# Gradient of w_down by seven block products, T4 late, a fourth staging buffer in the last group, Y transposed in the dxn loop

## The chip, the cores and the metric

The kernel runs on one core of one Trainium2 chip. The time is device microseconds of one execution of the whole program; the number used for a kernel is the median of its runs. Before the change three runs gave 796.46, 795.10 and 795.39 us: median 795.39. One more execution was recorded by the profiler, and all views below are of that one.

## The reference

A layer of linear attention with 32 heads and a SwiGLU feed-forward, with residuals, and its gradient. S = 2048 tokens, D = 640, F = 1728, all inputs bf16:

```python
h  = x + A(layernorm(x), wqkv, wo)            # linear attention, phi(t) = t+1 or exp(t)
h2 = h + (silu(hn @ w_gate) * (hn @ w_up)) @ w_down     # hn = layernorm(h)
_out, _vjp = jax.vjp(f, x, wqkv, wo, w_gate, w_up, w_down)
return (_out, *_vjp(grad_out))                # out_0, then dx, dwqkv, dwo, dw_gate, dw_up, dw_down
```

In the feed-forward's backward part, with g = hn @ w_gate and u = hn @ w_up, the kernel needs m = silu(g) * u, the gradients dg and du, and from them dw_down = m^T @ dh2 (dh2 is grad_out), dw_gate = hn^T @ dg, dw_up = hn^T @ du and dhn = dg @ w_gate^T + du @ w_up^T.

## The kernel before

Tokens lie in 16 tiles of 128 rows; D is 5 blocks of 128. The program runs through stages: attention forward (ps_kvt, L534 among them), gradient through w_down (ps_dm, L417), then the **feed-forward backward stage**, then ps_dhn (L108, the gradient into hn), attention backward, the **dxn loop** (L1069) and the **tail** (out_0's product L1138, ps_dwv L127).

**The feed-forward backward stage** runs over four groups g = 0 to 3 of columns of F, of width w = 448, 448, 448 and 384. A group goes through eight pairs of token tiles, t = 0, 2, ... 14. Per pair PE makes pg (gate, L731) and pu (up, L736), 20 matmuls; ACT takes two sigmoids and two copies of them (L752 to L755); DVE's seven operations at L764 write m into m_s and [dg | du] into dd (dd[0] holds tiles 0 to 7, dd[1] tiles 8 to 15); for the last pair they stand in another order, with dg last. SP then transposes each token tile of dd into a staging buffer, stg (L767), and stores the buffer into scr_dT in DRAM (L720); a store is issued one tile behind its transpose. The staging buffers are three, in turn. SP also issues the loads of the next group's weights, wgu (L190); in group 0 that load is asked for at t = 2.

**dw_group** then makes the weight gradients of the group's w columns: dw_down (transposed, into scr_dwdT; the five row blocks of D against m_s), dw_gate and dw_up (the five row blocks of D against dd's two halves of columns). Before, all of dw_down and row block 4 of gate and up are plain products over 16 tiles, by dw() into PSUM tiles ps_dw (L806). Row blocks 0 to 3 of gate and up are one product of 2 x 2 blocks by the Strassen-Winograd scheme: seven block products (prod, L646) in place of eight. The blocks of hn are two row-block pairs by two token halves, hn_blk(m, k, u). The blocks of dd are B11 and B12 (gate and up columns of the first token half), B21 and B22 (second half). DVE makes the sums that it needs by tt (L642): S and S3 from hn (128 x 1024 elements each), and from dd the differences T1 = B12 - B11, T2 = B22 - T1, T3 = B22 - B12 and T4 = B21 - T2 (128 x 8w each). T1 and T2 overwrite B11, T3 overwrites B12; T4 is written into m_s, whose own products are done by then. Partial results go from PSUM to buffers by ACT (copy, L673) and DVE (tt), and from there to DRAM by POOL's queue.

Inside dw_group a manual schedule sets the order of PE, DVE and ACT as the code is written; SP's order is set by hand in the whole stage. An engine does its list in order. Outside, a scheduler interleaves: the first pg matmuls of the next group may stand ahead of the last product of dw_group.

After group 3, ps_dhn starts. It reads cols, four token tiles of scr_dT at a time, loaded by load_cols: before, load_cols(0) and load_cols(1) are both issued by ACT (L157), the first ahead of group 3's dw_group, the second behind it; the later ones are issued by POOL (L160).

**The dxn loop** runs over 16 token tiles. SP issues three transposes into a ring of tiles per iteration (L972, L973, L1044), read by PE's ps_dxn. At iterations 8 to 13 it issues one transpose more, of G from scr_GT (L938); at 14 that of KV (L1050), from 14 on the first ones of mT (L1028), which the tail reads. **In the tail** SP transposes the rest of mT and, two at a time between them, six pieces of Y from scr_Yt, which ps_dwv reads.

## Time and profile before

| | us |
|---|---|
| median of three runs | 795.39 |
| the profiled execution's own time | 795.63 |
| its span in the profile | 793.9 |
| group 0's weight gradients, first product to the next group's first pg | 172.25 to 214.62 |
| group 3's weight gradients, to the first ps_dhn | 401.03 to 437.43 |
| one iteration of the dxn loop | 5.43 |

What lies outside the span, 795.63 - 793.9 = 1.7 us, is start and end of the program. Every view is read in microseconds from the span's start. In the chain of work that ended last a row has its start, its length, the engine, the tile, the line and how many instructions it groups; in the groups of instructions, a row has the line, engine, operation, tiles with their shape, count, the busy time in all with the mean of one in ns, and the idle time before it. A matmul's row shows it from issue to its end, 346 ns at 448 columns; since they are pipelined, the pace in a stream is read from the length of a chain row over its count.

### The profile page before, as it was taken

The numbers are of one execution on the slowest core, as the hardware profiler recorded it, in microseconds if no ns is written. First come the engines' busy times: TensorE is split into PE (matmuls) and PEld (weight loads), VectorE is DVE, ScalarE is ACT, GpSimd is POOL, SyncE is SP. The second block draws the span as 40 slices with busy tenths as digits, with TensorE's granted clock in tenths as the row PEclk, the third lists the DMA queues.
The fourth block names the chain that finished last, engine by engine and source line by source line (L and its number), as shares of the span: only waits on it lengthen the run. The fifth ranks groups of instructions, "written<-read, shape, count | busy, mean of one in ns | idle before, by whom it ended". The sixth has DMA issues, their size and how long they took to land.

```text
span 793.9 us, 13612 instructions
## 1 busy us (share of the span) xinstructions
PE 788.4 (99%) x5308; PEld 509.0 (64%) x5308; DVE 568.2 (72%) x1014; ACT 288.0 (36%) x414; POOL 172.7 (22%) x306
## 2 busy tenths in 40 slices
PE   9999999999999999999999999999999999999998
PEld 7776566555555555555666777777777777777766
DVE  7989988894497548845875259999897366635873
ACT  6962532760284045501831123223313133324010
POOL 4610047411201110011042102111221121223230
PEclk9999999999999999999999999999999999999999
DMA  9799999999769977892797659876498869999995
GB/s 261 154 241 298 209 211 277 262 256 238 171 154 241 214 169 191 211 253 71 148 233 196 253 144 191 217 194 176 120 257 176 161 135 161 177 212 239 228 213 150
DMA packets 286625, 160.03 MB, mean 202 GB/s; under 512 B 241548, under 2 KB 275405, under 8 KB 286560
## 3 DMA queue, kind: packets, MB, share of 16 engines
q1 hardware_dynamic: 268832, 99.48, 61.7%
q0 software_dynamic: 14832, 54.36, 22.6%
q10 hardware_dynamic: 2896, 5.33, 2.0%
q8 instruction: 41, 0.67, 0.4%
q14 instruction: 24, 0.20, 0.1%
HBM read 47.60 MB, written 53.66 MB: 128 GB/s over the span
## 4 chain that ended last, share of the span: by engine, by line
PE 97%; SPq 1%; DMA 1%; DVE 0%; issue 0%
PE ps_dhn L108 15%; PE ps_dw L806 10%; PE ps_dxn L1069 8%; PE pg L731 7%; PE ps_wa L646 7%; PE pu L736 7%; PE ps_kq L305 6%; PE ps_dwqk L986 5%; PE ps_dm L417 5%; PE ps_oa L1138 3%; PE ps_wc L646 3%; PE ps_y L508 3%; PE ps_dk L108 3%; PE ps_gt L861 3%; PE ps_dp L108 3%; PE ps_a L571 3%
## 5 line engine op out<-in xcount | busy, mean ns | idle before, releaser
L108 PE MATMUL ps_dhn<-wgT,cols 128*128 128x320 bf16 x864 | 119.5, 299 | 0.0
L108 PEld LDWEIGHTS <-cols 128*128 128x128 bf16 x864 | 84.5, 98 | 32.9
L146 DVE CUSTOM_DVE_ANT_0 lb_a<-lb_dy,hn 128x640 bf16<-128x640 bf16 x32 | 26.4, 825 | 58.9 <-ACT lb_dy L144 58.9
L731 PE MATMUL pg<-wgu,hnT 128*128 128x448 bf16 (+1 forms) x320 | 63.6, 346 | 0.0
L736 PE MATMUL pu<-wgu,hnT 128*128 128x448 bf16 (+1 forms) x320 | 63.6, 346 | 0.0
L806 PE MATMUL ps_dw<-m_s,dh 128*128 128x448 bf16 (+1 forms) x320 | 60.4, 346 | 0.0
L1069 PEld LDWEIGHTS <-ring 128*128 128x128 bf16 x480 | 47.0, 98 | 18.2
L1069 PE MATMUL ps_dxn<-wqkvT,ring 128*128 128x320 bf16 x320 | 51.3, 299 | 0.0
L736 PEld LDWEIGHTS <-hnT 128*128 128x128 bf16 x320 | 31.3, 98 | 27.1
L806 PEld LDWEIGHTS <-dh 128*128 128x128 bf16 x320 | 31.3, 98 | 27.1
L731 PEld LDWEIGHTS <-hnT 128*128 128x128 bf16 x320 | 31.3, 98 | 27.0
L417 PEld LDWEIGHTS <-dh2T 128*128 128x128 bf16 x320 | 31.0, 98 | 25.1
L417 PE MATMUL ps_dm<-wdT,dh2T 128*128 128x448 bf16 (+1 forms) x240 | 46.5, 344 | 0.0
L144 ACT ACTIVATE lb_dy<-ps_dhn,rstd 128x640 bf16<-128x640 f32 x16 | 12.7, 794 | 91.7 <-PE ps_dhn L108 91.7
L305 PE MATMUL ps_kq<-wqk,xnT 128*128 128x320 bf16 x320 | 45.0, 300 | 0.0
L752 ACT ACTIVATE dd<-pg 128x896 bf16<-128x896 f32 (+1 forms) x32 | 28.5, 890 | 40.4 <-PE pg L731 38.0
L305 PEld LDWEIGHTS <-xnT 128*128 128x128 bf16 x320 | 31.2, 98 | 12.2 <-DVE xnT L352 0.2
L646 PEld LDWEIGHTS <-S 128*128 128x128 bf16 x256 | 25.0, 98 | 21.7
L772 POOL DMA_DIRECT2D scr_m<-m_s x16 | 12.1, 756 | 122.6 <-DVE m_s L764 122.6
L986 PEld LDWEIGHTS <-hn 128*128 128x128 bf16 x320 | 31.1, 98 | 11.9
L642 DVE TENSOR_TENSOR dd<-dd 128x3584 bf16<-128x3584 bf16 (+1 forms) x12 | 23.1, 1953 | 21.4 <-PE ps_wa L646 15.6
L150 ACT ACTIVATE lb_a<-hn,lb_k 128x640 bf16<-128x640 bf16 x32 | 29.5, 920 | 21.7 <-DVE lb_k L149 18.9
(205 smaller groups left out, 1524.7 us busy)
## 6 DMA issues: line engine op xcount, KB each, us to landing
scr_dT<-stg SPq DMA_DIRECT2D x48, 224.0 KB, 2.8
cols<-scr_dT POOLq DMA_DIRECT2D x6, 1728.0 KB, 8.6
scr_m<-m_s POOLq DMA_DIRECT2D x12, 448.0 KB, 4.7
cols<-scr_dT ACTq DMA_DIRECT2D x2, 1728.0 KB, 10.6
scr_dT<-stg SPq DMA_DIRECT2D x16, 192.0 KB, 2.2
scr_pq<-pqa SPq DMA_DIRECT2D x4, 640.0 KB, 4.4
scr_xnT<-xnT SPq DMA_DIRECT2D x4, 640.0 KB, 5.3
scr_pk<-pk SPq DMA_DIRECT2D x4, 640.0 KB, 4.5
```

The lines of the kernel that those rows point to most:

```text
L108: nc.tensor.matmul(ps[:, ci, :320], lhsT=lhs(k), rhs=rhs(k, *NCH[ci]), start=(start and k == 0), stop=(stop and k == n - 1))
L146: nc.vector.tensor_tensor_reduce(out=a[:], in0=dy[:], in1=xhat, scale=1.0, scalar=0.0, op0=ALU.mult, op1=ALU.add, accum_out=sums[:, 1:2])
L150: nc.scalar.activation(out=a[:], in_=xhat, func=ACT.Identity, scale=k[:, 1:2], bias=k[:, 0:1])
L305: nc.tensor.matmul(ps[:, ci, :320], lhsT=xnT[:, t, k, :], rhs=wqk[:, k, w0 + n0:w0 + n1], start=(k == 0), stop=(k == DT - 1))
L417: nc.tensor.matmul(ps[:, c, :w], lhsT=dh2T[:, kt, (t + c) * P:(t + c + 1) * P], rhs=wdT[:, kt, o:o + w], start=(kt == 0), stop=(kt == DT - 1))
L646: nc.tensor.matmul(out, lhsT=lhs[:, t, :], rhs=rhs[:, t, :], start=(first and t == 0), stop=(t == 7), skip_group_check=not first)
L731: nc.tensor.matmul(pg[:, c, :w], lhsT=hnT[:, kt, (t + c) * P:(t + c + 1) * P], rhs=wg[:, kt, 0:w], start=(kt == 0), stop=(kt == DT - 1))
L736: nc.tensor.matmul(pu[:, c, :w], lhsT=hnT[:, kt, (t + c) * P:(t + c + 1) * P], rhs=wg[:, kt, w:2 * w], start=(kt == 0), stop=(kt == DT - 1))
L752: sig = nc.scalar.activation(out=dg, in_=pg[:, :, :w], func=ACT.Sigmoid)
L806: nc.tensor.matmul(ps[:, c, :w], lhsT=lhs(t), rhs=rhs(t), start=(t == 0), stop=(t == ST - 1))
L986: nc.tensor.matmul(ps[:, ci, :320], lhsT=xn_r[:, t, i * P:(i + 1) * P], rhs=dq[t // 8][:, t % 8, n0:n1] if which == 0 else dk[:, t, n0:n1] ...
L1069: nc.tensor.matmul(ps[:, ci, :320], lhsT=lhs[:, i, :], rhs=rhs[:, i, n0:n1], start=(k == 0 and i == 0), stop=(k == 2 and i == DT - 1))
```

## The change

**1. Seven products for dw_down as well.** Row blocks 0 to 3 of dw_down become a second scheme of 2 x 2 blocks: E11, E12, E21, E22 are m_s's token halves by its column halves (h = w/2 columns), F1 to F4 the differences from them, sd and sd3 the sums of dh2. Its seven products have h columns each, and go to the quarter banks of one PSUM tile, ps_qd, by q(). All seven of the first scheme stay. F1 to F4 overwrite E blocks. Since m_s is in use longer, T4 now overwrites B21, dd's first-column block of the second token half, and comes later in DVE's list.

**2. Order and places.** Row block 4 of gate comes first in dw_group, then B11's products, then the last two tiles of that row block. The sums sd lie in spare ends of other buffers (tails). The work pool fpool has 7 buffers instead of 6; the zero pads lie in a tail, and their stores are issued at t = 4 of group 3.

**3. Staging in group 3.** One token tile of four is staged in a buffer of its own (a tail of dm3), so four are in turn, and stores are issued two tiles behind.

**4. Loads.** The load of group 1's weights is asked for at t = 12 instead of t = 2. load_cols(0) is issued inside group 3's dw_group, on POOL.

**5. Y.** G is transposed at iterations 3 to 8 of the dxn loop instead of 8 to 13, Y at iterations 8 to 13 instead of in the tail.

```diff
-        def dw_group(g, w, m_s, dd, dw, dwd_part, dgu_part):
+        def dw_group(g, w, m_s, dd, spare, dwd_part, dgu_part):
...
-            T1, T2, T3, T4 = B11, B11, B12, m_s[:, 0:8, :w]
+            T1, T2, T3, T4 = B11, B11, B12, B21
+            E11, E12 = m_s[:, 0:8, 0:h], m_s[:, 0:8, h:w]
+            E21, E22 = m_s[:, 8:16, 0:h], m_s[:, 8:16, h:w]
+            F1, F2, F3, F4 = E11, E11, E12, E21
...
-            dw([dwd_part(0), dwd_part(1)], nc.vector.tensor_copy, first=True)
-            dw([dgu_part(4, 0), dgu_part(4, 1)], copy)
...
-            dw([dwd_part(4)], nc.vector.tensor_copy)
...
-            dw([dwd_part(2), dwd_part(3)], nc.vector.tensor_copy)
...
+            def q(b, lhs, rhs, first):
+                for u in U:
+                    prod(qd[:, b, u * h:(u + 1) * h], lhs(u), rhs, first, u == 0)
...
+            plain(f1[:, 0, :w], dgu_part(4, 0), 0, ST - 2)
+            for u in U:
+                prod(pa[u][:, 0, :w], hn_(0, 0, u), B11, True)
+            plain(f1[:, 0, :w], dgu_part(4, 0), ST - 2, ST)
             tt(T1, B12, B11)
+            for u in U:
+                prod(pa[u][:, 1, :w], hn_(0, 1, u), B21, True)
...
+            plain(f1[:, 1, :w], dwd_part(4), 0, ST)
+            for u in U:
+                tt(sd[u], dh_(1, 0, u), dh_(1, 1, u), ALU.add)
...
+            if g == 3:
+                load_cols(0)
+            q(0, lambda u: dh_(0, 0, u), E11, True)
+            q(1, lambda u: dh_(0, 1, u), E21, True)
+            tt(F1, E12, E11)
+            s1d = fp("s1d")
+            copy(out=s1d, in_=both(0))
+            evd0 = fw("dwd0")
+            tt(quarter(evd0, 0), both(1), s1d, ALU.add)
+            for u in U:
+                tt(S3[u][:], hn_(0, 0, u), hn_(1, 0, u))
+            tt(F3, E22, E12)
...
             for u in U:
                 prod(pc[:, u, :w], S[u], T1, True)
...
+            q(1, lambda u: sd[u], F1, True)
             tt(T2, B22, T1)
+            tt(F2, E22, F1)
+            for u in U:
+                tt(sd[u], sd[u], dh_(0, 0, u))
+            for u in U:
+                tt(S[u][:], S[u][:], hn_(0, 0, u))
+            plain(pa[0][:, 1, :w], dgu_part(4, 1), 0, ST)
...
+            q(0, lambda u: sd[u], F2, False)
...
+            tt(F4, E21, F2)
             tt(T3, B22, B12)
             for u in U:
                 prod(pa[u][:, 0, :w], S[u], T2, False)
...
+            for u in U:
+                tt(S[u][:], hn_(0, 1, u), S[u][:])
+            ev = fw("dwev")
+            for u in U:
+                prod(pa[u][:, 0, :w], S3[u], T3, False)
+                tt(ev[:, u, :w], pa[u][:, 0, :w], p5[u], ALU.add)
...
+                tt(sd3[u][:], dh_(0, 0, u), dh_(1, 0, u))
...
+                prod(pc[:, u, :w], S[u], B22, False)
+            q(0, lambda u: sd3[u], F3, False)
...
+                tt(sd[u], dh_(0, 1, u), sd[u])
             tt(T4, B21, T2)
+            evd1 = fw("dwd1")
+            tt(quarter(evd1, 1), both(1), u3d, ALU.add)
...
+            for u in U:
+                prod(pa[u][:, 0, :w], hn_(1, 1, u), T4, False)
...
+            q(1, lambda u: sd[u], E22, False)
...
+            tt(quarter(evd0, 1), both(1), u2d, ALU.add)
+            store_d(evd0, 0)
+            q(0, lambda u: dh_(1, 1, u), F4, False)
...
                 if g == 0 and t == 2:
                     wait_for(sig, load_dh2())
+                if g == 0 and t == 12:
                     load_wgu(1)
...
-                    stg = stage()
+                    stg = tails["dm3"] if g == 3 and (t + c) % 4 == 3 else stage()
...
-                    if len(staged) > 1:
+                    if len(staged) > 1 + g // 3:
                         store_dT(g)
...
+            if 3 <= t < 3 + HG:
+                tr_cols(G[:, t - 3, :], scr_GT, OH[t - 3])
             if 8 <= t < 8 + HG:
-                tr_cols(G[:, t - 8, :], scr_GT, OH[t - 8])
+                tr_cols(Y[:, t - 8, :], scr_Yt, OH[t - 8])
...
-            for j in range(2):
-                tr_cols(Y[:, j, :], scr_Yt, OH[j])
...
-                for j in range(2 * p + 2, min(2 * p + 4, HG)):
-                    tr_cols(Y[:, j, :], scr_Yt, OH[j])
```

The sequence of the products on PE, in dw_group after the change, is: row block 4 of gate, B11's and B21's products, row block 4 of dw_down, the quarter products with E11 and E21, S x T1, sd x F1, row block 4 of up, sd x F2, S x T2, S3 x T3, S x B22, sd3 x F3, T4's product, sd x E22, and last, behind the first matmuls of what follows, F4's quarter product.

Three places show what moves. The first is DVE's list in group 0's dw_group, from the third difference on; dd<-dd of 128x8x448 are the T differences, m_s<-dd was T4, and dm_1273 is the spare tail that holds sd. Before:

```order
L642 TENSOR_TENSOR dd<-dd 128x8x448 x2
L808 CAST dwev<-ps_dw 128x896
L642 TENSOR_TENSOR m_s<-dd 128x3584
L642 TENSOR_TENSOR S<-hn,S 128x1024 x2
L642 TENSOR_TENSOR dwev<-ps_wc,m_s 128x896
L642 TENSOR_TENSOR m_s<-ps_wc,m_s 128x896
```

And after, from T3 on (dwd are the evictions of the quarter products, dh_1882 is dh2):

```order
L643 TENSOR_TENSOR dd<-dd 128x8x448
L643 TENSOR_TENSOR S<-hn,S 128x1024 x2
L643 TENSOR_TENSOR dwev<-ps_wa,p_2384 128x448
L643 TENSOR_TENSOR dwev<-ps_wa,p_2385 128x448
L643 TENSOR_TENSOR S_2490<-dh_1882 128x1024
L643 TENSOR_TENSOR S_2491<-dh_1882 128x1024
L643 TENSOR_TENSOR dm_1273<-dh_1882,dm_1273 128x1024 x2
L643 TENSOR_TENSOR dd<-dd 128x8x448
L643 TENSOR_TENSOR dwd_2532<-ps_qd,u3d 128x2x224
L643 TENSOR_TENSOR dwev<-ps_wc,m_s 128x448 x2
L643 TENSOR_TENSOR dwd_2362<-ps_qd,u2d 128x2x224
```

T4, which stood behind one eviction and ahead of the last S sums, now stands behind two sums of S, two evictions that read S3 x T3, and four sums of dh2.

The second is the same list from the last operation of the pairs (L764 before, L862 after) through T2, where T1 stands. Before:

```order
L764 TENSOR_TENSOR dd<-a,nsg 128x2x448
L808 CAST dwev<-ps_dw 128x896
L642 TENSOR_TENSOR S<-hn 128x1024 x2
L642 TENSOR_TENSOR S_2244<-hn 128x1024
L642 TENSOR_TENSOR S_2245<-hn 128x1024
L642 TENSOR_TENSOR dd<-dd 128x8x448
```

After, where m_s<-m_s are F1, F3 and F2 in turn:

```order
L862 TENSOR_TENSOR dd<-a,nsg 128x2x448
L643 TENSOR_TENSOR dd<-dd 128x8x448
L643 TENSOR_TENSOR S<-hn 128x1024 x2
L643 TENSOR_TENSOR dwev<-ps_wa,s_2297 128x448
L643 TENSOR_TENSOR dwev<-ps_wa,s_2300 128x448
L643 TENSOR_TENSOR dm_1273<-dh_1882 128x1024 x2
L643 TENSOR_TENSOR m_s<-m_s 128x8x224
L643 TENSOR_TENSOR dwd_2362<-ps_qd,s1d 128x2x224
L643 TENSOR_TENSOR S_2239<-hn 128x1024
L643 TENSOR_TENSOR S_2240<-hn 128x1024
L643 TENSOR_TENSOR m_s<-m_s 128x8x224
L643 TENSOR_TENSOR dd<-dd 128x8x448
```

T1 moved from the sixth place to the second, ahead of every sum; F1, the first quarter sum and the sd sums stand between it and T2.

The third is SP's list at the end of the kernel, where mT<-scr_m are the transposes that out_0's product reads. Before:

```order
L1056 DMA wd<-in_B_w_down_dram 128x13x640
L1058 DMA wd<-in_B_w_down_dram 64x640
L1028 DMA_TRANSPOSE mT<-scr_m 128x14x128 x5
L938 DMA_TRANSPOSE mats<-scr_Yt 128x1x640 x2
L1028 DMA_TRANSPOSE mT<-scr_m 128x14x128 x2
```

After, around iteration 8 of the dxn loop, where G and Y now both stand once in the same iteration:

```order
L1137 DMA_TRANSPOSE ring<-dk 128x5x128
L1031 DMA_TRANSPOSE mats<-scr_GT 128x1x640
L1031 DMA_TRANSPOSE mats<-scr_Yt 128x1x640
L1065 DMA_TRANSPOSE ring<-scr_pk 128x5x128
L1066 DMA_TRANSPOSE ring<-dq 128x5x128
```

No transpose of Y is left between those of mT; an iteration of the loop has four transposes from the fourth on, and this one five.

More of the change, by code (lines that the diff above doesn't have):

```diff
@@ L406 @@
                 f(*a)
+    tails = {}
     dm_t = {0: strips.tile([P, ST, GM], BF16, name="dm0", tag="S")}
@@ new lines, in u2, with cut, plain, out_plain @@
+            def u2(u):
+                return kept[:, 4 * u:4 * u + 4, 0:h // 2]
+            def cut(ap, r):
+                return ap.rearrange("p (r n) -> p r n", r=r)
+            def plain(out, part, t0, t1):
+                for t in range(t0, t1):
+                    nc.tensor.matmul(out, lhsT=part[0](t), rhs=part[1](t), start=(t == 0), stop=(t == ST - 1))
+            def out_plain(part, ev):
+                nc.gpsimd.dma_start(out=part[2][:, GO[g]:GO[g] + w], in_=ev)
+            sd = [cut(ap, 8) for ap in spare]
@@ L687, in dw_group @@
+            ev = fw("dwev")
             for u in U:
                 prod(pa[u][:, 0, :w], S3[u], T3, False)
[L689 to L698 removed]
@@ new lines, in dw_group @@
+            u3d = fp("u3d")
+            copy(out=u3d, in_=both(0))
+            for u in U:
+                tt(sd[u], dh_(0, 1, u), sd[u])
+            tt(T4, B21, T2)
+            evd1 = fw("dwd1")
+            tt(quarter(evd1, 1), both(1), u3d, ALU.add)
+            ec = fw("dwev")
+            for u in U:
+                prod(pa[u][:, 0, :w], hn_(1, 1, u), T4, False)
+                copy(out=ec[:, u, :w], in_=pa[u][:, 0, :w])
+            store(ec, 0, 1)
+            q(1, lambda u: sd[u], E22, False)
@@ L705, in dw_group @@
+            for u in U:
+                tt(cut(ev[:, u, :w], 4), cut(pc[:, u, :w], 4), u2(u), ALU.add)
+            store(ev, 1, 0)
+            tt(quarter(evd0, 1), both(1), u2d, ALU.add)
+            store_d(evd0, 0)
+            q(0, lambda u: dh_(1, 1, u), F4, False)
+            copy(out=quarter(evd1, 0), in_=both(0))
+            store_d(evd1, 1)
             if g == 3:
@@ L821 @@
             with tc.manual_schedule(engines={EngineType.PE, EngineType.DVE, EngineType.Activation}):
-                dw_group(g, w, m_s, dd, dw, dwd_part, dgu_part)
+                dw_group(g, w, m_s, dd, spare, dwd_part, dgu_part)
     wB.close()
```

146 lines of the change are left out of this document (77 added, 69 removed).

## The prediction

> **What bounds the kernel now.** I read the page's busy shares first, then the chain that ended last, then who waited for whom, and only then the stages that the change touches.
>
> ```profile
> span 793.9 us, 13612 instructions
> PE 788.4 (99%) x5308; PEld 509.0 (64%) x5308; DVE 568.2 (72%) x1014; ACT 288.0 (36%) x414; POOL 172.7 (22%) x306
> PEclk9999999999999999999999999999999999999999
> PE 97%; SPq 1%; DMA 1%; DVE 0%; issue 0%
> PE ps_warm L341 <- DVE ones L244: 1.1, 1, 1.1
> PE ps_dwv L127 <- DMA mats<-scr_Yt: 1.0, 1, 1.0
> ```
>
> PE is busy for 99% of the span at full granted clock, the chain is PE for 97%, and in the last two rows (the waits of PE) it waits twice in all. So a matmul less is time less, as long as nothing new makes PE wait; a faster engine beside it gives nothing.
>
> ```profile
> 172.25 12.11 PE ps_dw L806 x64
> ...
> 214.62 1.89 PE pg L731 x10
> ...
> 256.99 6.05 PE ps_wa L646 x32
> ...
> 401.03 10.40 PE ps_dw L806 x64
> ...
> 434.83 2.60 PE ps_wc L646 x16
> 437.43 29.34 PE ps_dhn L108 x216
> 628.94 4.08 PE ps_dxn L1069 x30
> 81.63 1.43 PE ps_kvt L534 x30
> ```
>
> These rows of the chain (start, length, count) show each weight-gradient stage as one unbroken stretch of PE: 172.25 to 214.62 in group 0, 401.03 to 437.43 in group 3. They also give the pace of a matmul by its width: 448 columns 12.11/64 = 189 ns, 384 columns 2.60/16 = 162 ns, 320 columns 4.08/30 = 136 ns, and ps_kvt (25 of 120 columns, 5 of 40, so 107 on the mean) 48 ns. All lie on one line of 0.416 ns per column.
>
> **The product of seven blocks.** Per group, 64 matmuls of width w (rows 0 to 3 of w_down's gradient) go, and 7 products x 2 row blocks x 8 = 112 of width w/2 come. No row has widths 224 or 192; the line puts them at 96 and 83 ns, and the rows on both sides (48 ns at 107, 136 ns at 320) bound them. Groups 0 to 2 each save 12.11 - 112 x 0.096 = 1.36 us, group 3 saves 10.40 - 112 x 0.083 = 1.1. Together **5.2 us less matmul**.
>
> ```profile
> L646 PEld LDWEIGHTS <-S 128*128 128x128 bf16 x256 | 25.0, 98 | 21.7
> ```
>
> A weight load shows as 98 ns, longer than the 96 and 83 ns of the new matmuls. ps_kvt ran at 48 ns with one load each, so I take loads as overlapped. The Trainium skill, TensorE: Matmul & The Clock Gate, section Back-to-back issue gap, says that in a stream of load and matmul pairs both set the spacing, about 81 ns at 128 columns and 131 ns at 512. Interpolated (an estimate from that page) 64 x 0.123 us would be replaced by 112 x 0.094, and each group would lose 2.6 us where the sum above has 1.36 gained. The rows here, 189 ns at 448 and 48 ns at 107, do not agree with it.
>
> **What the seven products add on DVE.** Four F differences, eight more 128x1024 sums and three quarter sums join DVE's list, in a fixed order, and PE's products wait for them. What of it lies beside PE and what does not is decided at a few points.
>
> ```profile
> 251.98 2.49 DVE L642 TENSOR_TENSOR S<-hn 128x1024 bf16<-128x1024 bf16 x4
> 260.06 2.02 DVE L642 TENSOR_TENSOR dd<-dd 128x3584 bf16<-128x3584 bf16 x1 [5.58 <-PE ps_wa L646]
> 197.11 3.95 DVE L642 TENSOR_TENSOR dd<-dd 128x3584 bf16<-128x3584 bf16 x2
> L642 DVE TENSOR_TENSOR dwev<-ps_wa,s 128x448 bf16<-128x448 f32 x6 | 3.7, 623 | 2.7 <-ACT s L673 2.5
> 414.07 1.76 DVE L642 TENSOR_TENSOR dd<-dd 128x3072 bf16<-128x3072 bf16 x1 [4.42 <-PE ps_wa L646]
> 415.88 0.56 DVE L642 TENSOR_TENSOR dwev<-ps_wa,s 128x384 bf16<-128x384 f32 x1
> 188.93 0.53 ACT L673 COPY s<-ps_wa 128x448 f32<-128x448 f32 x1 [3.63 <-PE ps_wa L646]
> L731 PE MATMUL pg<-wgu,hnT 128*128 128x448 bf16 (+1 forms) x320 | 63.6, 346 | 0.0
> ```
>
> Prices: a 1024 sum 0.60 apart (2.49 for four, whose ends overlap by 0.09), a T 2.02 (1.93 apart), an eviction sum 0.62 (0.53 apart), an F of 1792 elements about 1.0, by the line between 1024 and 3584 elements. DVE starts 0.04 after PE (260.06 against 256.99 + 3.03). A restart of PE costs about 0.2: a matmul lasts 346 ns at a pace of some 189, and that 0.16, hidden in a stream, shows.
>
> *T4, the last big difference (sum over dd's second half).* It now stands behind one eviction sum and four 1024 sums, all waiting for the product S3 x T3; until the product with T4, PE has only S x B22 and one quarter product: 3.03 + 1.54 = 4.57 us. DVE needs 0.04 + 0.53 + 2.40 + 2.02, with the restart 5.2. **PE waits 0.65 in each of groups 0 to 2.** In group 3 the sums don't shrink with w: 0.04 + 0.47 + 2.40 + 1.76 + 0.2 = 4.9 against 2.60 + 1.33: 0.95.
>
> *T3.* From the quarter products' end to T3's end DVE has one ACT copy, an eviction sum, six 1024 sums, F3, F2, F4, T2 and T3: 11.9 us with hand-overs, against 12.2 of products on PE: hidden by 0.3. In group 3 it is 10.9 against 10.4: 0.45 of wait.
>
> *The last quarter product* waits for an eviction sum behind the product before it (0.04 + 0.62 + 0.2); four matmuls of the next group's pg (0.76) stand between: 0.1 each, 0.3 in all.
>
> ```profile
> 249.66 0.63 DVE L764 TENSOR_TENSOR dd<-a,nsg 128x896 bf16<-128x896 bf16 x1
> 405.82 0.56 DVE L764 TENSOR_TENSOR dd<-a,nsg 128x768 bf16<-128x768 bf16 x1
> ```
>
> *The start of a group.* Before, 28 matmuls passed ahead of one that needs the last pair of m_s; now 30 pass ahead of one that needs the last pair of dd, DVE's very last gating operation (the rows above). Group 1 starts at 244.89 (256.99 less 64 x 0.189): 30 x 0.189 is 250.57, the operand is there at 250.29: no wait. Group 3: 401.03 + 30 x 0.162 = 405.9 against 406.38 + 0.2: **0.7 of wait**.
>
> *T1 in group 0.*
>
> ```profile
> 164.93 0.39 SPq L190 DMA_DIRECT2D wgu<-in_B_w_gate_dram  x1
> ...
> 184.65 1.22 SPq L767 DMA_TRANSPOSE stg<-dd  x1
> ...
> 187.64 2.02 DVE L642 TENSOR_TENSOR dd<-dd 128x3584 bf16<-128x3584 bf16 x1 [5.81 <-DMA stg<-dd]
> ...
> 198.25 1.28 SPq L767 DMA_TRANSPOSE stg<-dd  x1
> 199.58 0.58 SPq L720 DMA_DIRECT2D scr_dT<-stg  x1
> 200.26 1.27 SPq L767 DMA_TRANSPOSE stg<-dd  x1
> ```
>
> T1 overwrites dd's first half, so it waits for the eighth transpose of dd on SP (184.65). There six transposes took 20 us after the weight load at 164.93; undisturbed they go every 2.0 us (198.25 to 200.26). With that load moved from t = 2 to t = 12 the eighth should land at 181 to 182.5 instead of 187.6. Behind T1 stand two S sums (1.2), two eviction sums (1.07), two sd sums (1.2) and F1 (1.0): 6.4 with T1's 1.93, and they should be done when the first quarter products and ACT's copy of them are, at 172.25 + 12.1 + 32 x 0.096 + 0.6 = 188, since from there to T3 DVE has 0.3 to spare (above). So T1 may start at 181.6; at 187.6 it would be 6 late and PE would wait 5.7. I take 0.4, near the undisturbed pace; bounds 0 and 5.7, the upper only if the moved load does not speed the transposes at all.
>
> **The other parts.** *Y in the dxn loop* takes the 1.0 us wait of ps_dwv away: its six transposes leave the tail, where they stood between the mT transposes on SP. What is late next there is nothing that PE waits for now.
>
> ```profile
> 660.37 1.24 SPq L1044 DMA_TRANSPOSE ring<-dk  x1
> ...
> 665.80 1.22 SPq L1044 DMA_TRANSPOSE ring<-dk  x1
> ```
>
> In the dxn loop SP has four transposes per 5.43 us and is nearly full; now iterations 3 to 7 also carry four, 9 to 13 still four and iteration 8 five, so SP falls back by 1.3 us. The ring is three tiles deep (over 10 us) and hides it; uncovered it costs 1.3.
>
> *load_cols(0)* goes from ACT to POOL behind an eviction, *load_cols(1)* on ACT behind the last copy of group 3.
>
> ```profile
> 411.38 0.40 ACTq L157 DMA_DIRECT2D cols<-scr_dT  x1
> 435.03 0.37 ACTq L157 DMA_DIRECT2D cols<-scr_dT  x1
> cols<-scr_dT POOLq DMA_DIRECT2D x1, 1728.0 KB, 10.9
> mats<-scr_W2T SPq DMA_DIRECT2D x1, 800.0 KB, 13.4
> ```
>
> The first stays near 412 and is needed at 437. The second goes from 435.03 to some 438.2; behind the two loads that run then (10.9 and 13.4 to landing) it is there by 451.6, and ps_dhn needs it two tiles (14.7) after 437.4, at 452.1: hidden, thinly. The fourth staging buffer, the seventh work buffer and the earlier zero stores work on SP and POOL beside PE: nothing, and what the buffer hastens is needed only for T4.
>
> **The sum**, against the profiled execution's own 795.63: -5.2 (matmuls) -1.0 (Y) +1.95 +0.95 (T4) +0.45 (T3) +0.3 (last quarter) +0.7 (group 3's start) +0.4 (T1) = -1.45, so 794.2. The median of the runs shown is 0.24 lower; I predict **794.0**. A measurement of this kernel tells about 0.2% (1.6 us) from no change, and this lies at that edge.
>
> **The rivals.**
> 1. *DVE is not late.* If PE's waits on T4, T3 and the group's start are covered, as every such wait is today (group 3's T3 by only 0.5), the 4.75 us vanish: 789.2; with half of them, 791.5. For it: DVE's row has 28% idle. Against: its order is fixed, and the idle time lies elsewhere. 0.15.
> 2. *The transposes become the bound (slower).* T4 used to write m_s; now it overwrites dd's second half and waits for the sixteenth transpose.
>
> ```profile
> 203.53 1.96 SPq L720 DMA_DIRECT2D scr_dT<-stg  x2
> 427.81 1.81 SPq L720 DMA_DIRECT2D scr_dT<-stg  x2
> 200.00:205.00 5.00, 5.00 (x29) 2.54 (x26) 3.51 (x3) 0.53 (x1) 1.06 (x2) 1.00 0.98 234
> ```
>
> The last stores behind those transposes go at about 204.9 and 429; T4 is due at 205.6 in group 0 and 431.2 in group 3. With the DMA engines full (0.98 in the last row) and the weight load now ahead of the last four transposes, 3 us more would cost 2.3 and 1.0: 797.3. It decides from a landing after 205.6. 0.16.
> 3. *Narrow products go at the pace of their weight load*, 98 ns: the saving falls from 5.2 to 3 x 1.13 - 0.6 = 2.8: 796.4. Against it stands ps_kvt. The page named above would have a larger loss still. 0.05.
> 4. *The moves do nothing*: PE's wait for Y is replaced by one for mT or cols of the same size: 795.0. 0.09.
>
> **How the numbers follow.** Forecast 0.55 (its own range 792.2 to 796, half of it below 793.8), rivals 0.15, 0.16, 0.05, 0.09. Faster by over 0.2% is half of the forecast and rival 1: 0.42. Slower is rival 2 and half of rival 3: 0.18. The rest, 0.40, is within. The range 790.0 to 797.8 leaves out the lower half of rival 1 and the upper tail of rival 2.
>
> **What would show it.** Right: waits of PE ps_wa on DVE dd of 0.5 to 1 us once in each group, one of PE ps_dw on DVE dd at group 3's start, 112 narrow matmuls in 10.8 us, no wait for scr_Yt. Wrong: no PE wait on DVE at all (rival 1), DVE waiting on stg<-dd before T4 (rival 2), narrow matmuls near 98 ns (rival 3), a PE wait on cols, mT or ring (rival 4).

## The result, and the profile after

| | us |
|---|---|
| before, median of 4 runs beside the change | 795.25 (794.5 to 796.46) |
| changed, median of 4 runs | **804.15** (802.81 to 805.12) |
| ratio | 1.0109 [1.009, 1.0129] |
| profiled execution: before, changed | 795.63, 802.81 |
| span of it: before, changed | 793.9, 801.1 |

The changed kernel is 1.1% slower; 794.0 was forecast, with a range up to 797.8. Single executions of it differ by up to 14 us, those of before seldom by 5, so the tables below give the fastest run and the number of runs more than 5 us above it beside the median; the ratios leave the most disturbed runs of both kernels out, and four executions of over 1000 us (two of "T4 earlier", one each of "four edits" and "the sums ahead of T1") are in no median here.

The first view of the changed kernel's page is the span, the busy shares and the chain by engine:

```profile
span 801.1 us, 14111 instructions
PE 786.4 (98%) x5500; PEld 524.8 (66%) x5500; DVE 599.2 (75%) x1070; ACT 297.8 (37%) x434; POOL 173.9 (22%) x307
PE 75%; DVE 12%; DMA 8%; issue 2%; SPq 1%; POOL 1%; ACT 0%; DVEq 0%; POOLq 0%; ACTq 0%
```

PE's busy time fell by only 2.0 us and the span grew by 7.2: PE now waits some 9 us more than before. The chain, PE for 97% before, now runs through DVE and DMA for a fifth. The waits of PE (what waited, for whom, total us, times, longest) say for what:

```profile
PE ps_oa L1233 <- DVE h1r L1217: 3.1, 1, 3.1
PE ps_wa L647 <- DVE dd L643: 2.8, 5, 0.9
PE ps_qd L647 <- DVE dwd L643: 2.5, 2, 1.3
PE ps_warm L344 <- DVE ones L247: 1.1, 1, 1.1
PE ps_qd L647 <- DVE dm L643: 1.0, 1, 1.0
PE ps_dw L683 <- DVE dd L862: 0.4, 1, 0.4
```

In PE's timeline (start, length, engine, line, operation; in brackets the idle time before it and its releaser) each stands at its place:

```profile
191.39 1.69 PE L647 MATMUL ps_qd<-m_s,dm 128*128 128x224 bf16 x16 [1.20 <-DVE dwd L643]
197.14 1.71 PE L647 MATMUL ps_qd<-m_s,dm 128*128 128x224 bf16 x16 [1.03 <-DVE dm L643]
210.21 3.19 PE L647 MATMUL ps_wa<-dd,hn 128*128 128x448 bf16 x16 [0.56 <-DVE dd L643]
282.32 3.19 PE L647 MATMUL ps_wa<-dd,hn 128*128 128x448 bf16 x16 [0.56 <-DVE dd L643]
369.56 3.19 PE L647 MATMUL ps_wa<-dd,hn 128*128 128x448 bf16 x16 [0.56 <-DVE dd L643]
407.28 0.48 PE L683 MATMUL ps_dw<-dd,hn 128*128 128x384 bf16 x2 [0.44 <-DVE dd L862]
422.02 1.50 PE L647 MATMUL ps_qd<-m_s,wgT 128*128 128x192 bf16 x16
423.35 2.76 PE L647 MATMUL ps_wa<-dd,S 128*128 128x384 bf16 x16
426.37 2.77 PE L647 MATMUL ps_wa<-dd,S 128*128 128x384 bf16 x16 [0.25 <-DVE dd L643]
433.93 2.76 PE L647 MATMUL ps_wa<-dd,hn 128*128 128x384 bf16 x16 [0.87 <-DVE dd L643]
437.96 1.48 PE L647 MATMUL ps_qd<-m_s,wgT 128*128 128x192 bf16 x16 [1.27 <-DVE dwd L643]
754.48 1.19 PE L1233 MATMUL ps_oa<-ot,os 128*128 128x320 bf16 x7 [3.08 <-DVE h1r L1217]
```

Six rows are those that the prediction named, at its size: T4 in four groups (0.56 three times and 0.87, each with the 0.16 of a restart: 0.72 and 1.03 for 0.65 and 0.95), T3 in group 3 (0.25 + 0.16 for 0.45) and group 3's start (0.44 + 0.16 for 0.7). The seventh named term, the last quarter product, is a gap too short for a bracket: in group 0 PE's row of four pg matmuls starts at 214.76 and the product's at 215.64, 0.12 more than 4 x 0.189, and with groups 1 and 2 it is 0.3 in all. The pace of the narrow matmuls is in the rows without a bracket: from 422.02 to 423.35 sixteen go, 83 ns each, as forecast.

The others are the loss. The first two stand behind T1 in group 0; with a restart of 0.16 each they are 2.55 us where 0.4 was put. The row at 437.96 is a quarter product that waits for a sum on DVE: 1.27 + 0.16, not in the prediction. The last is in the tail, also not in it. Behind that one the windows (stretch; busy us and instructions of PE, PEld, DVE, ACT, POOL; granted clock; DMA share; GB/s) show a second price:

```profile
751.00:754.40 3.40, 0.40 (x3) 0.16 (x2) 0.96 (x3) 0.00 (x0) 0.00 (x0) 1.00 1.08 155
754.40:757.00 2.60, 2.52 (x13) 1.59 (x13) 1.85 (x5) 0.00 (x0) 0.12 (x1) 0.69 1.20 328
757.00:759.00 2.00, 2.00 (x10) 1.16 (x8) 1.02 (x2) 0.00 (x0) 0.96 (x2) 0.55 1.19 185
759.00:761.00 2.00, 2.00 (x17) 1.47 (x15) 1.65 (x3) 0.00 (x0) 1.14 (x3) 1.00 1.18 336
```

After 3 us of rest PE gets little more than half its clock until 759: the 21 matmuls from 754.48 to 759.0 took 4.52 us, where they take 21 x 0.136 = 2.85. The wait of 3.08 cost 3.08 + 1.67 = 4.75.

With these the time is accounted for: -5.2 (narrow products) - 1.0 (Y) + 3.2 (T4) + 0.4 (T3) + 0.3 (last quarter) + 0.6 (group 3's start) + 2.55 (T1) + 1.43 (group 3's quarter) + 4.75 (tail) = +7.0, against 7.2 measured.

What releases the last two can be followed in the trace. For the quarter product of group 3, POOL's timeline:

```profile
426.49 0.72 POOL L160 DMA_DIRECT2D cols<-scr_dT  x1 [14.16 <-DMA scr_dT<-dm]
427.19 0.57 POOL L686 DMA_DIRECT2D out_dram<-dwev  x1
427.76 0.54 POOL L686 DMA_DIRECT2D scr_dwdT<-dwev  x1
428.29 0.54 POOL L686 DMA_DIRECT2D out_dram<-dwev  x1
428.82 0.54 POOL L653 DMA_DIRECT2D out_dram<-dwev  x1
```

And from the timeline of all engines, ACT's copy and DVE's sum of that product:

```profile
436.00 0.48 ACT L782 COPY u3d<-ps_qd 128x384 f32<-128x384 f32 x1 [9.37 <-DMA scr_dwdT<-dwev]
437.35 0.56 DVE L643 TENSOR_TENSOR dwd<-ps_qd,u3d 128x384 bf16<-128x384 f32 x1 [3.47 <-DMA out_dram<-dwev]
```

POOL stood at load_cols(0) for 14.16 us. It waits for a store out of dm (the last one that SP issues out of the fourth staging buffer, at 423.87), since cols takes the place of that buffer's strip: the edit that added the buffer and the one that moved the load meet there. Four stores of weight gradients stood behind it and then go back to back, so their work buffers come free late, and the two rows show ACT and DVE idle until a store out of dwev has landed. The product itself was done at 433.06 (431.58 + 1.48), so of ACT's 9.37 us only the last 2.9 are lost to that store. For the tail, the chain of waits:

```profile
731.63 8.45 DMA h1r<-scr_h
...
740.36 12.95 DMA h1r<-scr_h
```

Loads of h1r, 160 KB each, took 8.45 and 12.95 us; their median from issue to landing is 6.4 in this execution, 6.9 before. No edit of the change is on these loads.

### The profile page after: what moved, and what is told of

Same layout as the page of the kernel before. It is cut to its first block, busy times and chain, and to the rows that moved or that the text cites. A ratio compares the mean times of both kernels' runs of the same rounds, so it can differ in the third digit from the quotient of the medians.

```text
span 801.1 us, 14111 instructions
## 1 busy us (share of the span) xinstructions
PE 786.4 (98%) x5500; PEld 524.8 (66%) x5500; DVE 599.2 (75%) x1070; ACT 297.8 (37%) x434; POOL 173.9 (22%) x307
## 4 chain that ended last, share of the span: by engine, by line
PE 75%; DVE 12%; DMA 8%; issue 2%; SPq 1%; POOL 1%; ACT 0%; DVEq 0%; POOLq 0%; ACTq 0%
PE ps_dhn L108 15%; PE ps_dxn L1164 8%; PE ps_dm L421 5%; PE ps_dwqk L1079 4%; PE ps_wa L647 4%; PE pg L828 4%; PE pu L833 4%; PE ps_kq L308 4%; PE ps_qd L647 3%; PE ps_oa L1233 3%; PE ps_gt L954 3%; PE ps_dp L108 3%; PE ps_y L514 3%; PE ps_dk L108 3%; DMA h1r<-scr_h 3%; PE ps_a L577 3%
## 5 line engine op out<-in xcount | busy, mean ns | idle before, releaser
L647 PEld LDWEIGHTS <-S 128*128 128x128 bf16 x320 | 30.7, 98 | 21.9 <-DVE dd L643 1.1
L647 PE MATMUL ps_wa<-dd,hn 128*128 128x448 bf16 (+1 forms) x192 | 37.0, 346 | 2.6 <-DVE dd L643 2.6
L643 DVE TENSOR_TENSOR dd<-dd 128x3584 bf16<-128x3584 bf16 (+1 forms) x16 | 31.2, 1953 | 9.2 <-DMA stg<-dd 7.3
L862 DVE TENSOR_TENSOR m_s<-m_s,dd 128x896 bf16<-128x896 bf16 (+1 forms) x32 | 19.3, 604 | 21.4 <-ACT m_s L855 21.4
```

The costliest lines, as they stand in the source:

```text
L643: nc.vector.tensor_tensor(out=out, in0=in0, in1=in1, op=op)
L647: nc.tensor.matmul(out, lhsT=lhs[:, t, :], rhs=rhs[:, t, :], start=(first and fresh and t == 0), stop=(t == 7), skip_group_check=not (firs ...
```

## The experiments

Three questions: do these waits come from the edits they seem to come from, is the tail's wait the work of the Y move, and why does T1 come late. "Before" was run beside each kernel on the same chip. Letters in the expectations stand for theories and are explained there. Each row but the first has one profile, of one of its executions. Four kernels that are not in the table stand in the text.

| kernel | fastest | median | ratio to before | runs over 5 us above the fastest |
|---|---|---|---|---|
| before, on four chips | 793.67 | 794.73 to 794.9 | 1 | 9 of 150 |
| changed, again | 794.19 | 797.5 | 1.004 [1.0011, 1.0069] | 5 of 12 |
| Y back in the tail | 794.99 | 799.21 | 1.0034 [1.0011, 1.0056] | 4 of 11 |
| before with the Y move alone | 794.23 | 794.62 | 0.9995 [0.9984, 1.0005] | 0 of 11 |
| the same on another chip | 793.89 | 794.57 | 0.999 [0.9979, 1.0001] | 0 of 12 |
| three staging buffers | 794.04 | 798.62 | 1.0036 [1.0011, 1.0061] | 6 of 12 |
| load_cols(0) on SP | 794.08 | 795.78 | 1.0024 [0.9998, 1.0049] | 4 of 12 |
| T4 earlier | 791.27 | 797.16 | 1.0024 [0.9997, 1.005] | 5 of 10 |
| h1r ahead | 794.85 | 801.35 | 1.0056 [1.0029, 1.0084] | 8 of 12 |
| four staging buffers in group 0 | 794.01 | 796.73 | 1.0019 [0.9994, 1.0045] | 3 of 12 |
| weight load back at t = 2 | 796.35 | 798.28 | 1.0062 [1.0031, 1.0093] | 4 of 12 |
| four edits | 790.14 | 792.44 | 0.9978 [0.9951, 1.0004] | 4 of 11 |
| five edits | 789.79 | 791.49 | 0.9978 [0.9949, 1.0006] | 5 of 12 |
| six edits | 789.92 | 790.49 | 0.9956 [0.9929, 0.9983] | 3 of 12 |
| six edits, another chip | 789.81 | 790.31 | 0.9938 [0.9922, 0.9953] | 0 of 6 |

**The changed kernel again**, unedited, to see how much of the loss is fixed.

> The changed kernel itself, on the same chip and in the same rounds as the three kernels beside it. Theory G: the waits of PE in dw_group (0.56 on T4 three times, 0.87 on T4 and 0.25 on T3 and 0.44 on the last pair in group 3) are fixed by the order on DVE and come back to 0.05, while the single long waits (3.1 for h1r, 1.2 and 1.0 behind T1, 1.27 in group 3) depend on when transfers land and differ from run to run; the times spread over several us, 797 to 805, median 801 to 804, and a run with a wait of 3 us shows the clock below 1. Rival H: the 3.1 us for h1r are the change's own, at the same place in each run, and the times lie within 2 us of 804.

Five runs lie at 794.19 to 796.88 (794.19, 794.73, 794.95, 796.87, 796.88), five at 803 to 808. In the profiled one T4, T3 and group 3's start wait to the hundredth as above (0.56 three times, 0.87, 0.25, 0.45), T1's two waits are 0.61 and 1.03, group 3's quarter 0.66, and the tail does not wait. So the terms of DVE's order are fixed, and T1, the quarter and the tail move from execution to execution. At their best they cost nothing, and the time is the forecast one. Over these twelve the kernel is 0.4% slower than before, not 1.1.

**Y back in the tail; the Y move alone on before.** The first undoes the move in the changed kernel, the second makes it in before.

```diff
-            if 3 <= t < 3 + HG:
-                tr_cols(G[:, t - 3, :], scr_GT, OH[t - 3])
             if 8 <= t < 8 + HG:
-                tr_cols(Y[:, t - 8, :], scr_Yt, OH[t - 8])
+                tr_cols(G[:, t - 8, :], scr_GT, OH[t - 8])
...
+            for j in range(2):
+                tr_cols(Y[:, j, :], scr_Yt, OH[j])
...
+                for j in range(2 * p + 2, min(2 * p + 4, HG)):
+                    tr_cols(Y[:, j, :], scr_Yt, OH[j])
```

> The changed kernel, with Y's six transposes back between mT's in the tail and G's back at iterations 8 to 13. Theory A: without Y's short transposes between them, thirteen transposes of mT stand back to back, the loads of h1r share the DMA engines with them and one lands 13.0 us after its issue; PE waits 3.1 us for it and then runs 21 matmuls in 4.5 us instead of 2.85. With Y back that wait and the slow matmuls go (4.7 us) and the 1.0 us wait for Y returns: 804.15 - 3.8 = about 800.4, no PE wait over 1.5 us in the tail and a clock of 1.00 throughout. Rival B: h1r is late because the whole tail comes 3.3 us later against transfers that were started before; then nothing of the 3.1 goes, and 804 to 805 stays.

> The kernel before with the fifth part of the change alone: G at iterations 3 to 8, Y at 8 to 13, none in the tail. Theory A: the wait of PE for h1r appears here as well, 2.5 to 4.7 us less the 1.0 us for Y: 796.8 to 799, with a stretch of PE at a lower granted clock behind it. Rival B: the move alone takes its 1.0 us wait away and adds nothing: 794.2.

> The kernel before with Y and G moved alone, once more on the chip of the three beside it. If the moved Y alone makes the tail wait for h1r, a few of twelve runs lie over 798 now; if it needs nothing else than chance, 794.2 to 796 as in its first eleven runs, 0.2 to 0.5 us below the kernel before.

With Y in the tail no wait on h1r shows, but waits for scr_Yt of 2.08 and 0.27 us do, again with a clock of 0.50 behind them (columns as in the windows above):

```profile
763.00:765.00 2.00, 2.00 (x10) 1.08 (x8) 0.29 (x1) 0.00 (x0) 0.00 (x0) 0.50 1.25 193
```

The move on before brings no tail wait at all, and none of 23 runs is late. That the Y move by itself makes h1r late falls. It gains 0.3 us there by both medians; the 1.0 of the prediction lies within the intervals.

**Three staging buffers in group 3.**

```diff
-                    stg = tails["dm3"] if g == 3 and (t + c) % 4 == 3 else stage()
+                    stg = stage()
...
-                    if len(staged) > 1 + g // 3:
+                    if len(staged) > 1:
```

> The changed kernel with three staging buffers in group 3, stores one tile behind, as in the other groups; load_cols(0) stays on POOL inside dw_group. Theory C: the fourth buffer lies in dm3, whose place cols(0) takes, so that load waits for the last store out of it (426.5) and the stores behind it on POOL's queue wait too, up to ACT's copy u3d and the quarter sum that PE waits 1.27 us for. Without it the load is issued at 412 to 415, that PE wait goes, T4 may wait a little longer for the last transposes: 802.2 to 803.2. Rival D: the load behind the transposes is not what holds POOL (it would wait for the stores of scr_dT anyway): 804 to 804.5, and the 14 us of POOL stay.

The wait of 1.27 at 437.96 is gone, as the meeting of the two edits would have it. Another comes, in PE's timeline:

```profile
437.25 4.17 PE L647 MATMUL ps_wa<-dd,hn 128*128 128x384 bf16 x16 [4.52 <-DVE dd L643]
```

T4 now starts at 435.44, most likely behind the last transpose of dd, which SP issues from 430.5 to 433.4 where it had issued it by 422.4; the profile itself names no releaser for the last 2.75 us. The product behind T4 takes 4.17 us instead of 2.76, with a granted clock of 0.50 behind the wait. In this execution the fourth buffer is missed; the fastest run of the kernel, 794.04, is no slower than the changed kernel's, so not each execution needs it.

**load_cols(0) on SP**, behind the last store of scr_dT, with the fourth buffer kept. (cols(p) reads two token tiles, scr_dT[2p:2p+2], not four as in the description of the kernel above.)

```diff
-            if g == 3:
-                load_cols(0)
...
             while staged:
                 store_dT(g)
+            if g == 3:
+                load_cols(0, lambda out, in_: nc.sync.dma_start(out=out, in_=in_))
```

> The changed kernel with load_cols(0) issued by SP behind the last store of scr_dT, not by POOL inside dw_group; the four staging buffers stay. Theory C: POOL's queue is free, so the stores behind it go at 413 to 432 as they come, ACT copies u3d at 433 at once, and PE's 1.27 us wait on the quarter sum in group 3 goes with its restart: 1.5 us less than the changed kernel beside it; cols still lands by 437. Rival I: the stores are slow for the DMA engines' load and not for the queue; then the wait stays.

POOL's stores go at once, the quarter product does not wait, and cols is there when ps_dhn needs it. T1 started at 181.6 in this execution and nothing waits behind it. One execution would not be enough, since the wait varies, but the profiles agree: in the eight in which POOL stands 13.7 to 14.5 us at load_cols(0), six have the wait on the quarter sum (0.21 to 1.81 us); in the nine in which POOL does not, none has it. So the 1.43 us come from the blocked queue, and how much of it is paid differs from execution to execution. The profiled execution again has the tail's wait, larger, in PE's timeline:

```profile
755.17 2.02 PE L1233 MATMUL ps_oa<-ot,os 128*128 128x320 bf16 x7 [7.34 <-DVE h1r L1217]
```

**The sums ahead of T1**, to give T1 time, and **T4 earlier**, ahead of the last pair of sd sums:

```diff
-            tt(T1, B12, B11)
...
+            for u in U:
+                tt(sd[u], dh_(1, 0, u), dh_(1, 1, u), ALU.add)
+            for u in U:
+                tt(S3[u][:], hn_(0, 0, u), hn_(1, 0, u))
+            tt(T1, B12, B11)
```

```diff
+            tt(T4, B21, T2)
             for u in U:
                 tt(sd[u], dh_(0, 1, u), sd[u])
-            tt(T4, B21, T2)
```

> The changed kernel with the S, sd and S3 sums (six of 0.6 us) ahead of T1 on DVE, where DVE idles 7.0 us in group 0. Theory E: in group 0 T1 lands at the same time, for the eighth transpose, but 3.6 us less stand behind it, so PE's waits of 1.20 (ps_qd on dwd) and 1.03 us (ps_qd on dm) go, with a restart of 0.2 each: 801.4 to 802. The other groups stay within 0.3. Rival F: T1's lateness only moves on, to the sums F1 to T3, and PE waits for one of those the same 2 us: 804.

> The changed kernel with T4 two places earlier on DVE, ahead of the last two sums of dh2 (sd). Theory: T4 then ends 1.2 us earlier, 0.6 ahead of its product in groups 0 to 2 and 0.3 in group 3, so the waits of 0.56 three times and 0.87 go with their restarts: 3.2 us less than the changed kernel beside it. In group 0 some of the wait may stay if the sixteenth transpose lands after 207. Rival: T4 waits for the transposes of dd's second half, not for DVE; then the waits stay and the time is that of the changed kernel within 0.5.

The first gave a median of 801.57 and a ratio of 1.0098 [1.007, 1.0125]. That lies in the forecast range by luck: T1's two waits went, but the sums, which depend on nothing late, were put up among the pairs of group 0, where DVE is full, and PE waits there 3.04 us for dd (L862); in the tail of that execution it also waits 3.13 us for a copy of dwo on ACT. So the time tells nothing on T1. With T4 earlier it went as expected in the trace: the four T4 waits are gone, the others of DVE's order stay, and the fastest run is 2.9 below the changed kernel's (791.27 against 794.19). The median shows no such gain (797.16 against 797.5), since five of ten runs are late here too. The 3.2 us of T4 are the price of two sums in a wrong place.

**Why is T1 late?** Three kernels: the weight load put back to t = 2; a fourth staging buffer in group 0 as well; and, for the tail, six loads of h1r ahead in place of four.

```diff
                 if g == 0 and t == 2:
                     wait_for(sig, load_dh2())
-                if g == 0 and t == 12:
                     load_wgu(1)
```

```diff
-                    stg = tails["dm3"] if g == 3 and (t + c) % 4 == 3 else stage()
+                    stg = tails["dm3" if g else "st0"] if g % 3 == 0 and (t + c) % 4 == 3 else stage()
...
-                    if len(staged) > 1 + g // 3:
+                    if len(staged) > 1 + (g % 3 == 0):
```

> The changed kernel with group 1's weight load asked for at t = 2 again. By the prediction's step the load delays the first eight transposes: the eighth lands at 187 to 188, T1 starts 3 us later than in the changed kernel, and PE waits 3 to 4 us more in group 0, with a lower clock behind it where one wait reaches 3 us: 800 to 804 even in undisturbed runs. Rival: the eighth transpose is held by something else, lands at 184 to 185 as in the changed kernel, and the time stays at 794 to 798.

> The changed kernel with the fourth staging buffer in group 0 as well, and its stores two tiles behind. Theory L: SP's transposes of dd in group 0 are held by the landing of each one before its store (three buffers, one tile behind); with four the eighth lands by 181, T1 starts by 181.6, and PE's waits behind T1 (0.6 to 1.2 and 1.0) go: 2 us less in each undisturbed run, 792.5 to 796. By rival K the runs over 800 go too. Rival M: the transposes are slow because the DMA engines are full (share 1.0 from 140 to 200); then the eighth still lands at 183 to 184.5, and nothing changes.

> The changed kernel with the loads of h1r two token tiles further ahead (six before the loop of the tail instead of four, then two per step as before). Theory J: the runs over 800 us are those in which PE waits 3 us or more for h1r in the tail; then at most one run in twelve stays over 800, where five in twelve of the changed kernel did, and the median is 795 to 796.5. Rival K: the long waits arise in group 0 behind T1 or in group 3; then the share of runs over 800 stays near five in twelve.

One row of DVE's timeline shows T1 in each: the changed kernel, the weight load at t = 2, and the fourth buffer in group 0.

```profile
184.31 2.03 DVE L643 TENSOR_TENSOR dd<-dd 128x3584 bf16<-128x3584 bf16 x1 [6.96 <-DMA stg<-dd]
```

```profile
186.35 2.03 DVE L643 TENSOR_TENSOR dd<-dd 128x3584 bf16<-128x3584 bf16 x1 [8.61 <-DMA stg<-dd]
```

```profile
180.27 2.03 DVE L644 TENSOR_TENSOR dd<-dd 128x3584 bf16<-128x3584 bf16 x1 [2.30 <-PE ps_wa L648]
```

The waits behind T1 follow its start: none at 180.3 and 181.6, 0.55 at 183.2 (Y back in the tail), 2.2 at 184.3, 3.8 at 186.35, and 4.9 at 187.34 (the profiled run with h1r ahead). The point from which it decides, put at 181.6, was right within a microsecond; the landing was not. The eighth transpose, from issue to landing in the chain that ended last, shows where the step went wrong. The changed kernel first, then the weight load at t = 2:

```profile
177.73 6.46 DMA stg<-dd
```

```profile
183.37 2.91 DMA stg<-dd
```

The moved load does what it was moved for: the eighth transpose is issued at 177.73, not at 183.37 or, before, at 184.65. But then it takes 6.46 us to land, where it took 2.91 and, before, 3.0 (T1's start at 187.64 less 184.65). So of some 6 us won at the issue 2 are left at T1's start, and 2.2 in the fastest runs. With a further staging buffer T1 waits for no transpose in this profile. But late runs remain: the profile with four buffers has a wait on h1r of 7.91 us in the tail, and the kernel with h1r ahead has none there and still 8 late runs of 12.

**Together.** Four edits: T4 earlier, cols on SP, the first S, eviction and sd sums ahead of T1, and the last two iterations' pairs in the order 0, 2, 4, 1, 6, 3, 5. Five: with four staging buffers in group 0. Six: with h1r ahead.

> The changed kernel with four edits: T4 earlier, load_cols(0) on SP, in dw_group the first eviction sums, S and sd ahead of T1 (behind the products, so that they can't be moved into the pairs), and the last pair's dg ahead of m. By the theories the waits of T4 (2.55 with 0.6 of restarts), of the quarter sum in group 3 (1.5), behind T1 in group 0 (2.2 with 0.3) and of the last pair in group 3 (0.44 with 0.2) go: 7.8 us less than the changed kernel beside it, and where its times were long for a wait of 3 us in the tail that stays as it falls. The forecast is 791.5 to 793.5 in undisturbed runs, faster than the kernel before by 0.2 to 0.4%. Rival: with PE's waits gone, the transfers of the tail and of ps_dhn start of the same time and PE waits for those instead; then 795 to 797.

> The version with six edits without the sixth (h1r's loads as in the changed kernel); Y stays in the dxn loop. The waits of dw_group are gone in it, so what is left over 794 us comes from the tail alone. If the moved Y makes the tail's wait for h1r likely, some third of the runs lies 5 to 10 us over the rest, and the next kernel (Y in the tail) has fewer. If the tail waits as seldom as in the kernel before (3 of 35 runs), at most two of twelve. Undisturbed runs 790 to 791 in either case.

> The same with Y's transposes back in the tail and G's at iterations 8 to 13. If Y's place is what makes h1r late: no run with a long wait for h1r, but a wait of 1 to 2 us for scr_Yt in each: 791 to 793, and as few runs over 797 as before has. If Y's place is not the cause: the same share of long runs as in the kernel beside it.

> The four edits of the faster version (T4 earlier, load_cols(0) on SP, the first eviction sums, S and sd ahead of T1, the last pair's dg ahead of m) with the fourth staging buffer in group 0 and h1r further ahead. Where both steady the two places that differ from run to run, the times lie at 789.5 to 792 with at most one run in twelve over 797: 0.4 to 0.6% faster than before. If only one of them is the cause, a third of the runs stays over 797.

> The version with six edits once more, on the same chip as the two beside it: 790 to 791 in undisturbed runs. If h1r further ahead matters, fewer long runs than the version without it; if it doesn't, the same share.

The page of the six edits, and then all of PE's waits:

```profile
span 788.5 us, 14092 instructions
PE 783.4 (99%) x5500; PEld 524.8 (67%) x5500; DVE 598.8 (76%) x1070; ACT 297.9 (38%) x434; POOL 173.5 (22%) x306
```

```profile
PE ps_warm L344 <- DVE ones L247: 1.1, 1, 1.1
PE ps_kq L308 <- DMA xnT<-xn: 0.4, 1, 0.4
PE ps_wa L648 <- DVE dd L644: 0.2, 1, 0.2
```

With the waits gone the savings stand: span 788.5 against before's 793.9, 5.4 less, which is 5.2 of the narrow products and 1.0 of Y less 0.4 (T3) and 0.3 (last quarter), that stay. That is rival 1 of the prediction, made by edits; at 0.4 to 0.6% below before it is the fastest version found. The intervals of the four and of the five edits include no change. In the profile of the four edits T1 is late (at 190.4, a wait of 4.96 us). A fourth staging buffer does not rule that out: in the second profile of the six edits, an execution of 793.48 us, T1 again waits for a transpose, and PE waits 1.68 us for T1 and 1.33 for T4.

```profile
186.92 2.02 DVE L644 TENSOR_TENSOR dd<-dd 128x3584 bf16<-128x3584 bf16 x1 [2.07 <-DMA dm<-dd]
```

The five edits with Y put back in the tail give 798.25, ratio 1.003 [1.0008, 1.0053], with this row in the profile:

```profile
756.45 0.28 PE L127 MATMUL ps_dwv<-stg,mats 128*128 128x120 bf16 x1 [2.67 <-DMA mats<-scr_Yt]
```

A likely reading, argued from this one profile: in the tail Y's transposes go at SP's pace, so what PE gains before them is lost waiting for Y, and the clock falls to 0.50 behind that wait. On the old kernel the move gains 0.3 us; on this one 6.8 of the median.

**T1 to T3 of group 0 into another tile**, dm0, on the five edits and with h1r ahead, so that T1 waits for no transpose:

```diff
             T1, T2, T3, T4 = B11, B11, B12, B21
+            if g == 0:
+                T1 = T2 = dm_t[0][:, 0:8, :w]
+                T3 = dm_t[0][:, 8:16, :w]
```

> The version with five edits (Y in the loop, h1r as in the changed kernel) with T1 to T3 of group 0 written into dm0, which is dead by then, not over dd: they wait for no transpose of dd. If the long runs come from group 0's transposes (T1 due by 181 to 185, landing between 180 and 190 from run to run), at most one of twelve is 5 us over the fastest, where five of twelve were without this edit. If they come from h1r in the tail, some five of twelve stay. Undisturbed runs 789.5 to 790.5.

> The same with h1r loaded two token tiles further ahead (six edits and dm0). If the tail is what is left in the kernel beside it, this one has fewer long runs than it; if neither has any, group 0 was the cause. Forecast for undisturbed runs 789.5 to 790.5, median 790.

Medians 794.27, ratio 0.9987 [0.996, 1.0014], and 793.56, 0.9982 [0.9957, 1.0007]; about half of the runs are late in both. So T1 alone is not the cause, and h1r ahead makes no clear difference either (6 late runs of 12 without it, 5 with it). The second one's profile is of the longest of its runs. Its timelines of PE and of DVE, and its windows:

```profile
215.44 2.77 PE L648 MATMUL ps_wa<-dd,hn 128*128 128x448 bf16 x7 [7.15 <-DVE dd L644]
```

```profile
213.36 2.02 DVE L644 TENSOR_TENSOR dd<-dd,dm 128x3584 bf16<-128x3584 bf16 x1 [7.70 <-DMA dm<-dd]
```

```profile
215.40:217.00 1.60, 1.56 (x5) 0.66 (x5) 1.60 (x3) 0.00 (x0) 0.00 (x0) 0.50 1.13 219
```

This is rival 2 of the prediction: T4 of group 0 waiting for the sixteenth transpose of dd, landed at 213 where 205.6 decides. SP's timeline, first of this kernel and then of the one without h1r ahead, shows where the delay began:

```profile
152.32 20.51 SPq L867 DMA_TRANSPOSE stg<-dd  x3
```

```profile
150.16 11.95 SPq L867 DMA_TRANSPOSE stg<-dd  x3
```

The first three transposes came through at 173 in the one and at 162 in the other: ten us between two executions of programs that are alike up to there. (In the late one PE also waits in the tail, 2.27 and 1.61 us for ACT's copies of dwv.)

The delay is not dd's alone. In the late execution the last transpose of hn, issued at 150.89, ahead of those of dd, takes 19.44 us to land, and the pieces of dh2, which POOL loads from 149 on, in the same stretch, are late as well. The issues of that load (size, median us to landing), in this execution and in the changed kernel's:

```profile
dh<-in_grad_out_dram POOLq DMA_DIRECT2D x4, 640.0 KB, 13.2
```

```profile
dh<-in_grad_out_dram POOLq DMA_DIRECT2D x4, 640.0 KB, 9.0
```

Both go together in all twenty profiles: in five that median is 11.5 to 13.8 us and SP issues the first store of a transposed tile at 168.5 to 173.3; in the other fifteen it is 6.4 to 10.5 us and the store goes at 162.0 to 165.9. No run moves the load of dh2, so whether it holds up the transposes, or something else holds up both, is not shown. One of the five is the old kernel with the Y move alone. Its T1:

```profile
191.80 2.02 DVE L642 TENSOR_TENSOR dd<-dd 128x3584 bf16<-128x3584 bf16 x1 [9.23 <-DMA stg<-dd]
```

T1 is 4.2 us later there than in before's profile, and PE waits for nothing: the first product that reads it starts at 194.01. So late transposes are not new. The change took away the slack that hid them: T1 was in time at 191.8 and is now due at 182.

## Why the prediction was wrong

- **The saving** (5.2) and the pace of 83 and 96 ns: right. Rival 3, narrow products at the pace of their loads, is refuted.
- **T4, T3, the last quarter, group 3's start** (4.35 together): right within 0.2, the same in each unedited execution. Rival 1 fell for the kernel as it was.
- **The undisturbed time**: the fastest executions, 794.19 to 794.95, are the forecast 794.2. The sum of the fixed terms was right; what failed is that it left out what varies.
- **"I take 0.4, near the undisturbed pace"** failed. The issue of the eighth transpose came 7 us earlier, as was meant, but its landing took 6.46 us where the step counted on about 3. T1 was taken to start near 181.6; in the seven profiles with the changed kernel's order and buffers there it started between 181.6 and 187.3, and it cost 2.55 in the profiled one, 0 to 4.9 in others. The bounds 0 and 5.7 held; the value was taken from their lower end on one profile.
- **"load_cols(0) ... The first stays near 412"** and **"work on SP and POOL beside PE: nothing"** failed: the load stood until 426.5 for the buffer's strip, and POOL's queue behind it cost 1.43. Where two tiles share a place was not looked up.
- **Rival 2** did not happen in the changed kernel's two profiles: T4 waits 0.56 and 0.87 there, by DVE's order. It is the same mechanism at T1, and with the other waits gone it shows at T4 of group 0 too (0.65, 1.33 and 7.15 us in three profiles). Its price was too small: a late transpose gave not 3.3 but up to 7.15 us, with slow matmuls behind it.
- **Rival 4**, a wait for mT or cols in place of Y's, did not happen: no profile of the changed kernel has a PE wait on mT, cols or ring.
- **The tail's wait on h1r** (4.75, the largest term of the loss) stood nowhere in the prediction. "What is late next there is nothing that PE waits for now" failed. Here the cause stays **open**: it isn't the Y move alone (0 of 23 late), and loading h1r earlier isn't shown to cure it (3 of 18 late runs with it and 5 of 12 without on the five edits, 5 of 12 and 6 of 12 with dm0, but 8 of 12 on the changed kernel). What the profiles add: in the two with the longest waits on h1r, 7.34 and 7.91 us, the stores of dwo in the same stretch are slow as well (medians 11.6 and 16.3 us to landing, 5.1 to 10.0 in all others), so it is not these loads alone. How the late runs divide among these places isn't settled either, since one execution of each was profiled.

## What to carry to other kernels

When PE is busy for 99%, a faster product is paid out only where all that feeds it keeps its slack: list for each new dependency on a transfer when it is due, how far its landing spreads between executions, and charge the middle of that spread, with the slow clock behind it, not the undisturbed pace. Slack that hid a late transfer is a cost of the edit that spends it. An edit that gives a tile a new use has to be followed to whoever takes its place next, and to the queue in which that one waits. Once the waits were found in the trace, six short edits of order and buffers turned 0.4 to 1.1% slower into 0.4 to 0.6% faster.
